# Seven first products by Strassen's scheme, and forward transforms of 512 columns, in an H3 and MLP kernel

## The chip, the cores and the metric

The kernel runs on one core of a Trainium2 chip. The metric is the device time of one execution in microseconds (us). Before the change it is 848.18 us, the median of three runs (847.58 to 848.95).

## The reference

A sequence of 2048 tokens with 640 features passes four layers: a gated long convolution (A), an MLP (B), then both again with the same weights.

```python
def _A_ref(q, k, v, shift_k, ssm_k, ssm_D):
    ...
    kv = k_shift * v                      # k_shift: short causal convolution of k, 4 taps
    ...
    y = (lambda x, s, axes=(-2,-1): jnp.fft.irfft2(x, s=s, axes=axes))(y_f, (1, L), axes=(1, 2))[:, 0, :S, :]
    y = y + kv * ssm_D[None, None, :]
    return q * y

def _B_ref(x, w1, w2):
    h = jnp.einsum("bsd,df->bsf", x, w1)
    zero = jnp.zeros_like(h)
    h = jnp.maximum(h, zero)
    return jnp.einsum("bsf,fd->bsd", h, w2)

x = A_q
x = x + _A_ref(_layernorm(x, axis=-1), A_k, A_v, A_shift_k, A_ssm_k, A_ssm_D)
x = x + _B_ref(_layernorm(x, axis=-1), B_w1, B_w2)
x = x + _A_ref(_layernorm(x, axis=-1), A_k, A_v, A_shift_k, A_ssm_k, A_ssm_D)
x = x + _B_ref(_layernorm(x, axis=-1), B_w1, B_w2)
```

w1 is 640 by 1728, w2 1728 by 640. The convolution of A has no state that depends on x, so its result y is the same in both A layers and is computed once.

## The kernel before

**MLP blocks.** Tokens go in eight chunks of 256 (NC = 8). A block (a, l) is the MLP of chunk a in layer l. `order` lists them: chunks 0 and 1 in halves of 128 tokens, then in pairs of chunks, so that the last four blocks are (6,0), (7,0), (6,1), (7,1). `prep` makes a block's input (two layernorms, gate with y, residual), splits it into a high and a low f16 part (tile `xh`) and transposes both by DMA on the SP queue into `xT` (L1149). `main` runs over seven pairs of 128 hidden features (NFP = 7, in the order JS = 0, 1, 2, 3, 6, 4, 5). For a pair j the first product (`mm1`, L1291 to L1294) takes three f16 matmuls for each of the five feature tiles and each half of the pair: w high on x high, w high on x low, w low on x high; 30 matmuls of 256 columns into one PSUM tile `h` (ring of two). ACT applies the relu and DVE makes the low part of the result. The second product of the pair before is issued behind the first product of this one (`second(*prev)`). In the last four blocks (WINO) the second product already follows Strassen's scheme in Winograd's form: `wprod` (L1214), seven products of 320 columns on sums of h (`ha`, `hs`, `gs`, `tp`) and on combined forms of w2 that `wcombine` makes from w2 once more loaded. `wplain` is the plain form, used for j = 6 and, at some places, for one more pair.

**Convolution.** 21 units of one or two feature tiles. `transform(u)` loads k, v and the filter, applies taps and gate (tile `acc`), makes sum and difference `sd`, transposes on PE (`pt`), and multiplies by cosine and sine matrices (`pr`, L700 or L464 to L466); the filter goes the same way (`pg`). Units of rank FA = 6 and above (15 of them) do `pr` in three passes on a high and a low part in a rounded f32 type (`mm3`); the filter does so from rank FG = 11 on, and `products` (`pq`) from FU = 7 on. `products(u)` multiplies and adds spectra of earlier chunks, read back from DRAM (`Ax`, `Gx`), on DVE (L790 to L794), transforms back and writes y. The last unit's DVE instruction at L884 also writes `gate`, a tile without data: instructions that read it wait until the convolution is over and its buffers are free.

**Order.** Nothing is issued as written. `Plan` collects every instruction with a cost and a class, schedules them on a model of the engines and queues, computes latest start times (`latest`) and repeats the scheduling with them; MOVES is a list of passes, each of which is either empty (compute latest times again) or a tuple that shifts the keys of some instructions by pseudo-random amounts. The order that comes out is fixed for every engine and for SP. Buffers are rings: a tile takes the next free buffer of its tag.

Of the kernel before, what the change touches and what calls it, by code (L numbers as in the profile page):

```python
# [21 lines left out]
P = 128  # L22
# [64 lines left out]
FG = 11  # L87
# [5 lines left out]
SIGNED = ()  # L93
# [8 lines left out]

PETAP = {}

ACTN = 3
SADD0 = 0
WINO = ((6, 0), (7, 0), (6, 1), (7, 1))
EARLY = 1
ONPOOL = ()


def fview(ap):
    return ap.bitcast(F32)

# [15 lines left out]
class Sub:  # L130
# [5 lines left out]
    @property  # L136
    def t(self):
        return self.view(self.parent.t)


class Ring:
    def __init__(self, pool, tag, bufs):
# [1471 lines left out]
```

## Time and profile before

| | |
|---|---|
| runs before, median (range) | 848.18 us (847.58 to 848.95) |
| span of the profiled execution | 849.9 us |
| mean granted TensorE clock | 0.997 |
| busy: PE, DVE, ACT | 838.4, 754.0, 494.9 us |
| PE instructions | 7761 matmuls, as many weight loads |
| HBM | 183 GB/s over the span |

The span is from the first to the last instruction of one execution. No time other than the span is shown of that execution; it is 1.7 us longer than the median of the runs. A line such as L1291 is a line of the kernel before. Sums of matmul durations are larger than the time that they take, since a matmul's duration reaches into the next one; the distance from start to start is what PE needs for it.

The page's slices of the span (each 21.2 us, digits are tenths):

```profile
PE   7999999999999999999999998999999999999998
DVE  6999999999999999999999998999889598755454
ACT  4898597447685756637467373564516386647331
```

### The profile page before, as it was taken

How to read it: one execution, taken by the hardware profiler on the slowest of the kernel's cores; microseconds unless marked ns; L12 is line 12 of the kernel's file. 1: busy time of each engine (PE TensorE's matmuls, PEld its weight loads, DVE VectorE, ACT ScalarE, POOL GpSimd, SP SyncE). 2: the span in 40 equal slices, each digit the busy share in tenths (PEclk: the TensorE clock that was granted, in tenths of full speed). 3: DMA queues.
4: the chain of work that ended last, by engine and by line, in shares of the span. 5: the costliest groups of instructions: out<-in, count | busy, mean ns of one | idle time of the engine just before them, and what ended most of it. 6: DMA issues, size and time to landing. Idle time of an engine off the chain costs nothing.

```text
span 849.9 us, 19692 instructions
## 1 busy us (share of the span) xinstructions
PE 838.4 (99%) x7761; PEld 667.5 (79%) x7761; DVE 754.0 (89%) x1423; ACT 494.9 (58%) x1152; POOL 43.8 (5%) x54
## 2 busy tenths in 40 slices
PE   7999999999999999999999998999999999999998
PEld 6987888888878777777777776777777788888886
DVE  6999999999999999999999998999889598755454
ACT  4898597447685756637467373564516386647331
POOL 0000000000001101001011001010100000000000
PEclk9999999999999999999999999999999999999999
DMA  9996867987999998986998969597886363110100
GB/s 304 391 329 205 259 200 229 282 306 217 328 286 268 293 271 233 267 245 190 260 261 196 255 199 178 154 210 253 251 257 228 107 200 79 32 32 1 33 32 32
DMA packets 134143, 177.47 MB, mean 209 GB/s; under 512 B 50593, under 2 KB 88097, under 8 KB 134050
## 3 DMA queue, kind: packets, MB, share of 16 engines
q1 hardware_dynamic: 125730, 165.72, 63.7%
q0 software_dynamic: 8320, 10.49, 8.2%
q8 instruction: 61, 1.00, 0.5%
q14 instruction: 32, 0.26, 0.1%
HBM read 121.44 MB, written 34.08 MB: 183 GB/s over the span
## 4 chain that ended last, share of the span: by engine, by line
PE 89%; DVE 5%; DMA 2%; ACT 1%; SPq 1%; issue 1%; DVEq 0%
PE h L1291 12%; PE h L1292 12%; PE h L1294 12%; PE o L1214 9%; PE o L1263 8%; PE o L1264 8%; PE o L1266 7%; PE oc L1263 2%; PE oc L1264 2%; PE oc L1266 2%; PE pg L659 1%; PE pq L845 1%; DMA hf<-in_hF 1%; DVE w L975 1%; PE hb L1291 1%; PE hb L1292 1%
## 5 line engine op out<-in xcount | busy, mean ns | idle before, releaser
L1292 PE MATMUL h<-xT,w 128*128 128x256 f16 (+1 forms) x1290 | 302.1, 252 | 2.4 <-DMA xT<-xh 2.4
L1291 PE MATMUL h<-xT,w 128*128 128x256 f16 (+1 forms) x1290 | 302.2, 252 | 0.0
L1294 PE MATMUL h<-xT,w 128*128 128x256 f16 (+1 forms) x1290 | 302.0, 252 | 0.0
L1292 PEld LDWEIGHTS <-w 128*128 128x128 f16 x1390 | 136.3, 98 | 22.9 <-DMA xT<-xh 2.7
L1291 PEld LDWEIGHTS <-w 128*128 128x128 f16 x1390 | 136.3, 98 | 21.7 <-issue 0.5
L1294 PEld LDWEIGHTS <-w 128*128 128x128 f16 x1290 | 126.5, 98 | 9.1
L794 DVE TENSOR_TENSOR pacc<-pacc,pd 128x768 f32<-128x768 f32 x140 | 132.6, 948 | 0.4
L1263 PE MATMUL o<-w,hh 128*128 128x512 f16 x336 | 127.3, 379 | 0.0
L1264 PE MATMUL o<-w,hh 128*128 128x512 f16 x336 | 127.3, 379 | 0.0
L1380 ACT ACTIVATE hh<-h 128x512 f16<-128x512 f32 (+1 forms) x98 | 47.2, 484 | 119.3 <-PE h L1294 112.3
L1264 PEld LDWEIGHTS <-hh 128*128 128x128 f16 x672 | 65.8, 98 | 26.8 <-issue 0.3
L1263 PEld LDWEIGHTS <-hh 128*128 128x128 f16 x672 | 65.7, 98 | 26.8 <-issue 0.2
L793 DVE TENSOR_TENSOR pd<-Ax,Gx 128x768 f32<-128x768 f32 x83 | 78.2, 948 | 1.6 <-DMA Gx<-G 1.5
L1266 PE MATMUL o<-w,hl 128*128 128x512 f16 x208 | 78.8, 379 | 0.0
L1263 PE MATMUL oc<-w,hh 128*128 128x128 f16 x336 | 73.9, 220 | 0.0
L1264 PE MATMUL oc<-w,hh 128*128 128x128 f16 x336 | 73.6, 219 | 0.1
L1266 PEld LDWEIGHTS <-hl 128*128 128x128 f16 x416 | 40.7, 98 | 24.5
L538 ACT ACTIVATE tp<-kt,shs 128x256 f32<-128x256 f32 (+1 forms) x78 | 42.9, 575 | 12.9 <-DVE acc L612 10.3
L1266 PE MATMUL oc<-w,hl 128*128 128x128 f16 x208 | 45.6, 219 | 0.0
L1381 DVE SCALAR_TENSOR_TENSOR hl<-h,hh 128x512 f16<-128x512 f32 x50 | 34.2, 683 | 11.5 <-ACT hh L1380 11.5
L793 DVE TENSOR_TENSOR pd<-at,Gx 128x768 f32<-128x768 f32 x46 | 43.2, 948 | 1.3 <-DMA Gx<-G 1.1
L1266 PE MATMUL o<-w,hh 128*128 128x512 f16 x104 | 39.4, 379 | 0.0
(247 smaller groups left out, 1748.4 us busy)
## 6 DMA issues: line engine op xcount, KB each, us to landing
Ax<-A SPq DMA_DIRECT2D x89, 384.0 KB, 4.5
Gx<-G SPq DMA_DIRECT2D x89, 384.0 KB, 4.5
A<-at SPq DMA_DIRECT2D x30, 384.0 KB, 5.4
G<-gt SPq DMA_DIRECT2D x30, 384.0 KB, 4.9
ws<-in_w SPq DMA_DIRECT2D x28, 320.0 KB, 6.5
y<-Y SPq DMA_DIRECT2D x22, 320.0 KB, 4.0
x<-in_q SPq DMA_DIRECT2D x16, 320.0 KB, 4.5
gs<-in_hF SPq DMA_DIRECT2D x20, 256.0 KB, 3.9
```

What stands on the lines that cost most here:

```text
L538: ACT.activation(o[:, i : i + m], kview(i, m, j), AF.Copy, scale=shs[:, t, j : j + 1])
L793: ew(f"mac{j % POOLMOD}", 768, lambda e, pd=pd, av=av, gv=gv: e.tensor_mul(pd.t, av(), gv()), [ax, gx], [pd], pr_)
L794: dve(768, lambda i=i, pd=pd: DVE.tensor_add(acc[:, i], acc[:, i], pd.t), [acc, pd], [acc], pr_)
L1214: PE.matmul(b[:, c : c + w], x, y[:, z : z + w], start=done[i] == 1, stop=end, skip_group_check=fin)
L1263: PE.matmul(z, hh[:, c], wh[:, d], start=(j == JS[0] and i == 0 and (h == 0 or s == S[0])), stop=False)
L1264: PE.matmul(z, hh[:, c], wl[:, d], start=False, stop=end and tail)
L1266: PE.matmul(z, hl[:, c], wh[:, d], start=False, stop=end)
L1291: PE.matmul(p[:, z], wh, xv(t, 0), start=b, stop=False)
L1292: PE.matmul(p[:, z], wh, xv(t, 1), start=False, stop=tail and e)
L1294: PE.matmul(p[:, z], wl, xv(t, 0), start=False, stop=e)
L1380: act(2 * R, lambda p=p, hh=hh: ACT.activation(hh.t, p.t, AF.Relu), [p], [hh], URGENT)
L1381: dve(2 * R, lambda p=p, hh=hh, hl=hl: DVE.scalar_tensor_tensor(hl.t, p.t, 0.0, hh.t, op0=ALU.max, op1=ALU.subtract), [p, hh], [hl], URGENT)
```

## The change

1. **First product.** For blocks (6,1) and (7,1) (`WINO1`) and the pairs of `J1` (4, 5, 3, 1, 2; in (6,1) only 4 and 5), `wfirst` takes the place of the two `mm1` calls. Tokens (two halves of 128), hidden features (two of 128) and input features (two of 256) form a 2 x 2 x 2 product done in seven products of 128 columns; the fifth feature tile is added in plain form. 54 matmuls of 128 columns go into two `h` tiles, and one ACT copy and five DVE additions recombine them into an SBUF tile `both`, from which the relu then reads.
2. **Forms of w1.** `w1combine`, called behind `wcombine`, loads the five pairs of w1 again (ten DMAs of 320 KB that wait for `gate`), combines them on DVE, scales and splits them on ACT and DVE into tiles that take over buffers of the finished convolution (`SLOTS`).
3. **Forms of x.** `prep` of these two blocks makes four combined token tiles on DVE, splits them and transposes them by four more DMAs into `tT` (in `kt`, `vt`, `hf`, `hr`). The partial sums of the second product move from these to `pacc`; `hs` and `ls` become halves of one tile in `gs`.
4. **Forward transforms.** In the three-pass form the matrices are reordered so that the two that differ by alternating signs share one weight: the signs are put on the moving columns (ACT copies scaled by `alt`), and 6 matmuls of 512 columns take the place of 12 of 256. On ACT one copy of 512 becomes six of 256, on the way out two copies of 512 become two of 256 and one of 512 (a third copy of 512, of some units, becomes two of 256); on DVE one subtraction of 512 becomes two of 256.
5. **FG from 11 to 9**: two more units' filter transforms take the three-pass form.
6. **Waits and buffers.** In block (6,0) the plain second products and the relu also wait for `gate`. `cM` is split for four matrices, not six, and sits, like `cG`, in a ring. The unused code for signed units goes, with its load `cN`.
7. **MOVES** is another list, longer (311 shifts for 86), so the whole order is planned anew.

```diff
-FG = 11
+FG = 9
+WINO1 = ((6, 1), (7, 1))
+J1 = (4, 5, 3, 1, 2)
+J1_AT = {(6, 1): (4, 5)}
+SLOTS = (("cs", 2), ("cs", 2), ("cg", 1), ("dl", 1), ("acc", 1), ("tp", 2), ("tp", 2), ("u", 2), ("u", 2), ("ag", NAG))
...
+            xh, xl = (T(cv, "rt", 2, [P, 2, h], f"s{x}" + nm, F32R) for x in "hl")
+            yh, yl = (T(cv, *r_, [P, 2, h], f"d{x}" + nm, F32R) for r_, x in ((("tp", 2), "h"), (("dl", 1), "l")))
+            for hi, lo, k in ((xh, xl, 0), (yh, yl, 1)):
+                act(h, lambda hi=hi, k=k: ACT.activation(hi[:, k], pv()[:, k], AF.Copy), [pt], [hi], pr_)
+                dve(h, lambda hi=hi, lo=lo, k=k: DVE.tensor_sub(lo[:, k], pv()[:, k], fview(hi[:, k])), [pt, hi], [lo], pr_)
+            for hi, k in ((xh, 1), (yh, 0)):
+                act(h, lambda hi=hi, k=k: ACT.activation(hi[:, k], pv()[:, k], AF.Copy, scale=alt.t), [pt, alt], [hi], pr_, 0.09)
+            for lo, src, k in ((xl, yl, 1), (yl, xl, 0)):
+                act(h, lambda lo=lo, src=src, k=k: ACT.activation(lo[:, k], fview(src[:, k]), AF.Copy, scale=alt.t), [src, alt], [lo], pr_, 0.09)
+
+            def f():
+                for i, (hi, lo) in enumerate(((xh, xl), (yh, yl))):
+                    mm3(pr[i][:, 0:w], cMs, i, hi.r("p a b -> p (a b)"), lo.r("p a b -> p (a b)"), True, True)
...
+    def w1combine():
...
+            dve(256, lambda b=b: DVE.tensor_add(b(1, 1), b(1, 1), b(1, 0)), [r1], [r1], CONV)
+            dve(256, lambda b=b: DVE.tensor_sub(b(1, 0), b(0, 0), b(1, 0)), [r0, r1], [r1], CONV)
+            dve(256, lambda b=b: DVE.tensor_sub(b(0, 0), b(1, 1), b(0, 0)), [r0, r1], [r0], CONV)
+            dve(256, lambda b=b: DVE.tensor_sub(b(0, 1), b(0, 1), b(0, 0)), [r0], [r0], CONV)
+            dve(P, lambda b=b: DVE.tensor_sub(b(0, 2), b(0, 2), b(1, 2)), [r0, r1], [r0], CONV)
...
+                act(512, lambda r=r, w=w: ACT.activation(w[:, 0], r[:, 0:512], AF.Copy, scale=s()), [r, sc[0]], [w], CONV, 0.09)
+                dve(512, lambda r=r, w=w: DVE.scalar_tensor_tensor(w[:, 1], r[:, 0:512], s(), w[:, 0], op0=ALU.mult, op1=ALU.subtract), [r, sc[0], w], [w], CONV, 0.13)
...
-                pe(0.136 * (6 if j < NFP - 1 else 5), f, [hh, hl, WT[j, 1, 0], WT[j, 1, 1]], [b for b, *_ in place(m)], FILL + 0.2 * ending)
+                pe(0.136 * (6 if j < NFP - 1 else 5), f, [hh, hl, WT[j, 1, 0], WT[j, 1, 1]] + [gate] * ((a, layer) == WINO[0]), [b for b, *_ in place(m)], FILL + 0.2 * ending)
...
+        def wfirst(j, pa, pb, c):
...
+            groups = (
+                (A, 0, ((plain_w(0, 0), tok(0, 0), 2),)),
+                (A, 1, ((form(f0, 0), comb(1), 2),)),
+                (A, 2, ((form(f1, 1), comb(0), 2), (a_(1), tail_x(1), 1))),
+                (A, 3, ((form(f1, 0), comb(2), 2),)),
+                (B, 0, ((form(f0, 1), tok(1, 1), 2), (ad, tail_x(1), 1))),
+                (B, 1, ((plain_w(1, 1), comb(3), 2), (a_(1), tail_x(0), 1))),
+                (B, 2, ((plain_w(0, 1), tok(0, 1), 2), (a_(0), tail_x(0), 1))),
+            )
...
+                    mms = [(w(kk, h), x(kk, l)) for w, x, n_ in parts for kk in range(n_) for h, l in ((0, 0), (0, 1), (1, 0))]
+                    for z, (y, x) in enumerate(mms):
+                        PE.matmul(p[:, k * P : k * P + P], y, x, start=z == 0, stop=z == len(mms) - 1)
...
+            act(P, lambda: ACT.activation(c[:, 3], at_(A, 0), AF.Copy), [A], [c], URGENT)
+            dve(P, lambda: DVE.tensor_add(c[:, 0], at_(A, 1), c[:, 3]), [A, c], [c], URGENT)
...
+            dve(256, lambda: DVE.tensor_add(c[:, 1:3], at_(A, 2, 2).rearrange("p (k e) -> p k e", k=2), once()), [A, c], [c], URGENT)
+            dve(P, lambda: DVE.tensor_add(c[:, 0], at_(B, 2), c[:, 3]), [B, c], [c], URGENT)
+            dve(P, lambda: DVE.tensor_add(c[:, 3], at_(A, 2), c[:, 2]), [A, c], [c], URGENT)
+            dve(256, lambda: DVE.tensor_add(c[:, 1:3], at_(B, 0, 2).rearrange("p (k e) -> p k e", k=2), c[:, 1:3]), [B, c], [c], URGENT)
...
-            mm1(j, 0, p)
-            p1 = T(ps, "h", 2, [P, 2 * R], f"hb{n}", stream=sm) if j == NFP - 1 else p
-            mm1(j, 1, p1)
+            seven = tT is not None and j in J1_AT.get((a, layer), J1)
+            if seven:
+                p1 = T(ps, "h", 2, [P, 2 * R], f"hs{n}_{j}", stream=sm)
+                both = T(cv, "rt", 2, [P, 4, P], f"ha{n}_{j}", stream=7)
+                wfirst(j, p, p1, both)
```

More of the change, by code (lines that the diff above doesn't have):

```diff
@@ L456, in csplit @@
     def csplit(t, k, ring=None, after=()):
-        hi, lo = (T(wp, "w", NW, [P, k, P], t.name + x, F32R, stream=2) if ring else keep(const, [P, k, P], t.name + x, F32R) for x in "hl")
-        act(k * P, lambda: ACT.activation(hi.t, t.t, AF.Copy), [t, *after], [hi], LATER)
-        dve(k * P, lambda: DVE.tensor_sub(lo.t, t.t, fview(hi.t)), [t, hi], [lo], LATER)
+        hi, lo = (T(*ring, [P, k, P], t.name + x, F32R, stream=2) for x in "hl")
+        act(k * P, lambda: ACT.activation(hi.t, t[:, 0:k], AF.Copy), [t, *after], [hi], LATER)
+        dve(k * P, lambda: DVE.tensor_sub(lo.t, t[:, 0:k], fview(hi.t)), [t, hi], [lo], LATER)
         return hi, lo
@@ L686, in transform @@
         pv = lambda: pt[:, 0:w].rearrange("p (a b) -> p a b", a=2)
-        sh = T(cv, "rt", 2, [P, 2, h], "sh" + nm, F32 if full else F32R)
-        act(w, lambda: ACT.activation(sh.t, pv(), AF.Copy), [pt], [sh], pr_)
-        if not full:
-            sl = T(cv, "rt", 2, [P, 2, h], "sl" + nm, F32R)
-            dve(w, lambda: DVE.tensor_sub(sl.t, pv(), fview(sh.t)), [pt, sh], [sl], pr_)
         at = T(*park, [P, n, 3, 256], "at" + nm, stream=1)
         pr = [R(f"p{ri}", [P, 512], f"pr{ri}" + nm) for ri in range(2)]
-        def f(ris):
-            for ri in ris:
+        third = by_dma and not c0
@@ L697, in f @@
+        if full:
+            sh = T(cv, "rt", 2, [P, 2, h], "sh" + nm)
+            act(w, lambda: ACT.activation(sh.t, pv(), AF.Copy), [pt], [sh], pr_)
+            def f(ri):
                 for kk in range(2):
                     o = pr[ri][:, 0:w].rearrange("p (c k e) -> p c k e", c=n, k=2)[:, :, kk, :]
-                    if full:
-                        PE.matmul(o, cMt[:, 2 * kk + ri, :], sh[:, ri, :], start=kk == 0, stop=kk == 1)
-                    else:
-                        mm3(o, cMs, 2 * kk + ri, sh[:, ri, :], sl[:, ri, :], kk == 0, kk == 1)
@@ L704, in transform @@
-        if full:
-            for ri in range(2):
-                pe(8 * mm4, lambda ri=ri: f([ri]), [sh, cMt], [pr[ri]], pr_)
-        else:
-            pe(12 * mm, lambda: f([0, 1]), [sh, sl, *cMs], pr, pr_)
-        for ri in range(2):
-            act(w, lambda ri=ri: ACT.activation(at[:, :, ri, :], pr[ri][:, 0:w].rearrange("p (c b) -> p c b", c=n), AF.Copy), [pr[ri]], [at], pr_)
-        if by_dma and not c0:
-            act(w, lambda: ACT.activation(at[:, :, 2, :], pr[0][:, 0:w].rearrange("p (c b) -> p c b", c=n), AF.Copy), [pr[0]], [at], pr_)
+                    PE.matmul(o, cMt[:, 4 * kk + ri, :], sh[:, ri, :], start=kk == 0, stop=kk == 1)
@@ L1322, in main @@
         if wino:
-            e1, u2, u3, v = (T(cv, x, 1, [P, H], f"e{x}{n}", stream=7) for x in ("kt", "vt", "hf", "hr"))
+            kept = T(cv, "pacc", 1, [P, 4, H], f"ek{n}", stream=7)
+            e1, u2, u3, v = (Sub(kept, lambda t, k=k: t[:, k]) for k in range(4))
             def res(s, h, src, t, z=0, w=H, last=False):
@@ L1547, in _consts @@
     cg = np.concatenate([cg, -cg[:, 2:4], -cg[:, 1:2]], 1)
-    cg = np.concatenate([cg, -cm[:, 1:2], -cm[:, 5:6]], 1)
-    return [x.astype(np.float32) for x in (cm, cg)]
+    return [x.astype(np.float32) for x in (cm, cg, row)]
 def _rows(x):
```

151 lines of the change are left out of this document (109 added, 42 removed), and 70 rows, old and new, of the table MOVES.

## The prediction

> **What bounds the kernel now.** I read the page's totals first, then a table of busy time by stretch, then the order of the matmuls one by one in the few places where the change puts its hand.
>
> ```profile
> span 849.9 us, 19692 instructions
> PE 838.4 (99%) x7761; PEld 667.5 (79%) x7761; DVE 754.0 (89%) x1423; ACT 494.9 (58%) x1152; POOL 43.8 (5%) x54
> ```
>
> A busy PE need not be a full PE, since its instructions overlap, so I counted steps from start to start. In the plain first product of the last blocks 60 matmuls of 256 columns lie between these two starts (the row behind them ends a full second product):
>
> ```profile
> 804.44 0.27 PE L1291 MATMUL h<-xT,w 128*128 128x256 f16 x1
> ...
> 810.99 0.43 PE L1214 MATMUL o<-w,hh 128*128 128x320 f16 x2
> ...
> 813.85 0.27 PE L1291 MATMUL h<-xT,w 128*128 128x256 f16 x1
> ```
>
> 6.55 us / 60 = 0.1092 us each, and the seven 320-column products that follow take 2.86 us. PE issues without a hole. The stretches say the same (from:to, length, then PE, PEld, DVE, ACT, POOL busy):
>
> ```profile
> 100.00:650.00 550.00, 547.23 (x5063) 426.56 (x5061) 534.49 (x905) 321.28 (x763) 41.96 (x40) 1.00 0.88 246
> 676.00:720.00 44.00, 44.00 (x407) 37.43 (x405) 37.23 (x84) 32.23 (x70) 0.00 (x0) 1.00 0.54 162
> 720.00:803.00 83.00, 83.00 (x745) 69.46 (x744) 49.24 (x140) 46.33 (x111) 0.00 (x0) 1.00 0.11 25
> 803.00:846.00 43.00, 42.75 (x379) 35.38 (x377) 22.62 (x57) 11.14 (x21) 0.00 (x0) 1.00 0.06 20
> ```
>
> From 100 us on PE sets the end. DVE is nearly full too up to 650 us (534.5 of 550) and has room only in the last four blocks. PE's one large hole behind the start is here:
>
> ```profile
> 517.80 0.81 DVE L1137 TENSOR_TENSOR xh<-xnB,xh 128x640 f16<-128x640 f32 x1
> 519.61 7.28 DMA xT<-xh
> 526.94 0.28 PE L1292 MATMUL h<-xT,w 128*128 128x256 f16 x1 [2.35 <-DMA xT<-xh]
> 527.00:529.00 2.00, 2.00 (x14) 1.59 (x15) 1.45 (x5) 0.00 (x0) 0.00 (x0) 0.72 0.62 208
> 529.00:531.00 2.00, 2.00 (x12) 1.41 (x10) 0.00 (x0) 0.00 (x0) 0.00 (x0) 0.50 0.00 0
> ```
>
> The block at 524 us has its input split late on the full DVE (517.80), the transposing DMA lands 7.28 us later, PE idles 2.35 us, and then the granted clock (the seventh figure behind the length) is 0.72 and 0.50. A mean of 0.72 is 1.12 of 2 us at half rate; with the 2 us behind it that is 3.1 us at half rate, 1.6 us lost. The hole costs 2.35 + 1.6 = 3.9 us. The Trainium skill ("TensorE: Matmul & The Clock Gate", part 1 on the HAM clock gate) has the clock halved only after an idle window of about 3.4 us; this trace differs, 2.35 us of idleness was enough here. By the page the hole would be worth 2.35 us alone.
>
> **The change, part by part.** PE first.
>
> First product of seven feature pairs (two in block (6,1), five in (7,1)). Removed: 30 matmuls of 256 columns, 30 x 0.1092 = 3.28 us. Added: 54 of 128 columns (27 into each of two PSUM tiles). Their step stands in the half blocks, where the same pattern (two streams on one weight, then the low weight) runs 30 at a time:
>
> ```profile
> 163.68 0.38 PE L1264 MATMUL o<-w,hh 128*128 128x512 f16 x1
> 163.90 0.38 PE L1266 MATMUL o<-w,hh 128*128 128x512 f16 x1
> 164.11 0.22 PE L1291 MATMUL h<-xT,w 128*128 128x128 f16 x1
> ...
> 165.73 0.22 PE L1294 MATMUL h<-xT,w 128*128 128x128 f16 x1
> 165.76 0.36 PE L464 MATMUL pr<-sh,cMh 128*128 128x256 f32 x1
> 165.96 0.29 PE L465 MATMUL pr<-sl,cMh 128*128 128x256 f32 x1
> ...
> 167.16 0.28 PE L466 MATMUL pr<-sh,cMl 128*128 128x256 f32 x1
> 167.28 0.23 PE L1263 MATMUL oc<-w,hh 128*128 128x128 f16 x1
> ```
>
> 29 steps in 1.62 us: 0.0559 each, 54 make 3.02 us. 7 x 0.26 = **1.8 us less**. It is near one tenth of the multiplications, since the fifth tile of features keeps its plain form, and twice as many instructions each carry about 3 ns.
>
> The Trainium skill speaks against this part: the same page, section "Back-to-back issue gap", gives 81 ns for a sustained stream of weight load and matmul at 128 columns, far over the 56 of one matmul alone. The row above disagrees: it is such a stream, each matmul with its own load, at 56. By the page 54 would be 4.4 us, an estimate, and each pair a loss of 1.1.
>
> Forward transforms. The group from 165.76 to 167.28 is the old form: 12 matmuls of 256 columns, 1.52 us, 0.120 a step from 165.96 on, and 0.08 more on the first. The new form is 6 of 512 over the same columns. No such row with this type exists. From below it is the f16 step at 512 columns (163.68 to 163.90: 0.215), from above twice the old step (0.240). I take 0.22, nearer the lower, because in f16 doubling the columns halves the fixed part. That is 0.08 + 6 x 0.22 = 1.40, 0.12 less (0 to 0.15). It runs in 15 units:
>
> ```profile
> L464 PE MATMUL pr<-sh,cMh 128*128 128x256 f32 x60 | 18.8, 313 | 0.0
> 78.07 1.95 PE L659 MATMUL pg<-gs,cG 128*128 128x256 f32 x8
> 79.85 0.22 PE L1263 MATMUL oc<-w,hh 128*128 128x128 f16 x1
> ```
>
> (60 of this kind, four a unit.) 15 x 0.12 = **1.8 us less** (0 to 2.2). FG from 11 to 9 moves two units' filter transform from 8 full-precision matmuls (78.07 to 79.85: 1.78 us) to the 12-matmul form (1.52): **0.5 us less**.
>
> Now what the other engines get. DVE and ACT, by start-to-start steps and means:
>
> ```profile
> 513.13 0.68 DVE L691 TENSOR_TENSOR sl<-pt,sh 128x512 fp32r<-128x512 f32 x1
> 513.73 0.94 DVE L794 TENSOR_TENSOR pacc<-pacc,pd 128x768 f32<-128x768 f32 x1
> ...
> 641.07 0.41 DVE L883 TENSOR_TENSOR ys<-pq,qs 128x256 f32<-128x256 f32 x1
> 641.40 0.95 DVE L794 TENSOR_TENSOR pacc<-pacc,pd 128x768 f32<-128x768 f32 x1
> ...
> 665.88 0.68 DVE L852 TENSOR_TENSOR ul<-u,uh 128x512 fp32r<-128x512 f32 x1
> 673.56 0.47 PE L464 MATMUL pq<-uh,cMh 128*128 128x256 f32 x1
> 676.14 0.41 DVE L884 TENSOR_TENSOR ys<-pq,qs 128x256 f32<-128x256 f32 x1
> ```
>
> On DVE each of the 15 units trades a 512 subtraction (0.60) for two of 256 (0.33 each): +0.06 x 15 = 0.9. FG adds 2 x 2 x 0.60 = 2.4. So 3.3 us more before the convolution ends. The cover: the last unit's operands are ready at 665.88 + 0.60 = 666.5 and PE takes them at 673.56, 7.1 us later, because it still has block (5,1) to do. PE will be there 2.3 us sooner and DVE 3.3 later; 1.5 us are left, so I cost it at nothing. Were the cover gone, the gate (written at 676.14) would be late, and with it three engines' queues: on SP the w2 and w1 loads and behind them the inputs of (7,0); on ACT the relu of (6,0)'s second pair and behind it the copies that its split needs; on PE the second product of its first pair and behind it the next first product. PE would idle by as much as the gate is late, each microsecond one for one, and by 1.6 more once it has idled 2.35.
>
> ```profile
> L880 ACT ACTIVATE qs<-pq 128x256 f32<-128x256 f32 x19 | 7.2, 376 | 17.8 <-PE pq L466 17.2 <-PE pq L845 0.5
> L710 ACT ACTIVATE at<-pr 128x512 f32<-128x512 f32 x38 | 22.1, 587 | 10.5 <-PE pr L466 5.9 <-PE pr L700 4.1
> ```
>
> On ACT a unit had one copy in and two out (3 x 0.59 = 1.8 us). It gets six of 256 in, two of 256 and one of 512 out (8 x 0.376 + 0.59 = 3.6): +27 us over 15 units, +2 for the third part of ten of them, +2.5 for FG. ACT goes from 321 to about 352 of 550 us, and these copies are behind no matmul that is due at once; nothing, as long as the order keeps the relus of the MLP first.
>
> The last four blocks. The forms of w1 cost DVE, per pair, four passes of 256, one of 128, two scalings of 512, one of 128; a prep with tT four of 256 and two of 512; the recombination three of 128 and two of 256:
>
> ```profile
> 815.68 0.60 ACT L1367 ACTIVATE ha<-h 128x512 f32<-128x512 f32 x1 [1.87 <-PE h L1294]
> 816.31 0.29 DVE L1371 TENSOR_TENSOR hs<-ha 128x128 f32<-128x128 f32 x1 [1.78 <-ACT ha L1367]
> ...
> 818.65 0.69 DVE L1378 TENSOR_TENSOR tp<-hs,gs 128x512 f16<-128x512 f32 x1 [0.69 <-ACT gs L1376]
> ...
> 840.30 0.69 DVE L1381 SCALAR_TENSOR_TENSOR hl<-h,hh 128x512 f16<-128x512 f32 x1 [2.52 <-ACT hh L1380]
> 840.91 0.48 DVE L1340 TENSOR_TENSOR evt<-o,ekt 128x320 f32<-128x320 f32 x1
> ```
>
> With 0.41, 0.29 and 0.69: 4 x 0.41 + 0.29 + 2 x 0.69 + 0.29 = 3.6, times five 18.0; preps 2 x 3.0 = 6.0; recombination 1.7 a pair, 3.4 in (6,1) and 8.5 in (7,1). From 720 to 803 us that is 27.4 us into 83 - 49.2 = 33.8 us of room; in the last block 8.5 into 20.4. The ten loads and eight transposes meet an almost idle DMA (share 0.11), and on SP they stand ahead only of the other transposes of a block that starts some 40 us later. The chain behind a first product, relu to last low part, is now 815.68 to 819.34, 3.7 us; three DVE passes more behind the second PSUM tile make it 4.7. It is needed after the second product before it (2.86) and the next first product (3.02), 5.9 us later: covered, with 1.2 us over. Its two PSUM tiles come free about 1 us behind their last matmul, inside those 2.86.
>
> The end: there DVE runs one pass after another from 840.30. Three passes more (1.0 us) fall just before, where it has 2.5 us idle, but the low part of the last pair comes 1 us later and pushes what follows. I take **+0.2 us** (0 to +0.8).
>
> The sum is -1.8 - 1.8 - 0.5 + 0.2 = -3.9 us on a span of 849.9: 846.0. The median of the runs lies 1.7 us under that span, what lies around the span included; carried over, 848.18 - 3.9 = **844.3 us**.
>
> **The rivals.** The whole order is planned anew, so the hole at 524 us is not bound to return, and another can open.
>
> *No hole.* The new order brings that block's split before 515 us, or the landing is short. Then another 3.9 us go: 840.4. For it: one late DVE pass and one slow landing made it. Against: DVE gets fuller in that stretch, and the runs' median, 1.7 us under the profile, may lack part of it already. Chance 0.21.
>
> *One hole more.* Where DVE is full, another block's input or the gate comes 2.4 us late: +3.9, 848.2, no change. For it: 1.5 us of cover left before the gate. Chance 0.17.
>
> *DVE takes over in the last blocks* (the other side). It decides from the point where forms, splits and recombinations together outrun the 33.8 us of room between 720 and 803: at 27.4 added DVE would be 92% full there, and a recombination queued behind a 0.69 scaling or two is late by more than the 1.2 us that its chain has over. If each of the seven pairs makes PE wait by one form pass and its hop, about 0.8, plus one half-clock spell of 1.6, the cost is 7.2: 848.18 - 3.9 + 7.2 = 851.5. Against: before 650 us the kernel runs at 97% DVE with one hole. Chance 0.13.
>
> *Weight loads bind the 128-column stream.* A load takes 98 ns:
>
> ```profile
> L1292 PEld LDWEIGHTS <-w 128*128 128x128 f16 x1390 | 136.3, 98 | 22.9 <-DMA xT<-xh 2.7
> ```
>
> At one per load 54 make 5.3 us, +2.0 a pair, 14 in all: 848.18 + 14 - 2.1 = 860. That is how the skill's 81 ns would act; the rows at 164 us speak plainly against it. Chance 0.02.
>
> **How the numbers follow.** My forecast, the arithmetic with the waits as they are, has 0.47; its own range is 842.5 (transforms at their best, half a hole less) to 846.4 (transforms gain nothing). The range 839.9 to 849.2 takes in the case without a hole and that with one more, and leaves the two slow cases out. 0.2% is 1.7 us, about what a measurement of this kernel tells from no change, so faster is under 846.5: 0.47 + 0.21 = 0.68. Within: 0.17. Slower: 0.15.
>
> **What would show it.** Steps right: 54-matmul groups at 0.056 a step; pr groups of six at 0.21 to 0.24; pg groups of eight in two units fewer; PE without idle rows between 676 us and the end, DVE there above 85%. Wrong: PE idle rows in front of o or h matmuls released by DVE in the last two blocks, or by xT or tT landings; a half clock behind them; a pq group of the last unit that follows its ul pass at once, which says that the cover at the gate is gone.

## The result, and the profile after

| | before | after |
|---|---|---|
| runs, median (range), 22 each | 848.42 us (846.89 to 851.91) | 849.44 us (848.04 to 852.50) |
| ratio to before, 95% interval | | 1.0016 (1.0009 to 1.0024) |
| span of the profiled execution | 849.9 us | 847.2 us |
| that execution's own time | not known | 849.02 us |

The change costs 1.0 us; 844.3 was forecast. The two profiled spans say the opposite of the runs, and the reason comes first. Every listed execution of these two kernels that has both figures has its time 1.7 to 1.9 us over its span (849.02 over 847.2 here). The median of the runs before, 848.42, belongs to a span near 846.6. The profiled execution of before, at 849.9, was some 3 us longer than the usual one, so its hole at 524 us can hardly be in most runs (an inference: only profiled executions show their waits).

The lines of the page after, and the stretches of the trace (from:to, length, then PE, PEld, DVE, ACT, POOL busy, granted clock, DMA share, GB/s):

```profile
span 847.2 us, 20204 instructions
PE 835.9 (99%) x7847; PEld 661.0 (78%) x7847; DVE 788.2 (93%) x1529; ACT 534.3 (63%) x1282; POOL 43.8 (5%) x54
DVE  7999999999999999999999999999998789989775
ACT  4898687557785666667466466564725377678531
100.00:650.00 550.00, 545.94 (x4978) 418.31 (x4976) 535.71 (x919) 347.98 (x865) 42.02 (x40) 1.00 0.87 243
720.00:803.00 83.00, 83.00 (x808) 70.54 (x807) 71.22 (x202) 57.43 (x134) 0.00 (x0) 1.00 0.29 66
803.00:843.00 40.00, 40.00 (x480) 34.29 (x477) 28.91 (x79) 10.91 (x23) 0.00 (x0) 1.00 0.06 22
```

The last blocks look much as forecast: PE never idles, and DVE is 86% full from 720 to 803 us (71.22 of 83), where 92% was forecast. In the middle, from 100 to 650 us, ACT has risen from 321 to 348 us, DVE is as full as before, and PE idles 4.1 us instead of 2.8. The waits of PE (engine, line, what it waited for; us in total, times, longest), without those of the start:

```profile
PE h L1378 <- DMA xT<-xh: 2.4, 3, 1.1
...
PE pt L726 <- ACT ob L706: 0.7, 1, 0.7
PE h L1377 <- DVE hh L1535: 0.5, 1, 0.5
...
```

The first row is three inputs of blocks, at 320, 476 and 527 us. The chain that leads to the one at 476 us (start, us, what), and the matmul that waited:

```profile
464.89 0.75 DVE xh L1206
465.64 0.60 DVE gt L707
466.24 0.87 DVE pacc L853
467.11 0.60 DVE gt L708
467.71 0.73 DVE xh L1206
...
470.92 6.52 DMA xT<-xh
477.48 0.27 PE h L1378
```

```profile
476.09 0.28 PE L1377 MATMUL h<-xT,w 128*128 128x256 f16 x1
477.48 0.27 PE L1378 MATMUL h<-xT,w 128*128 128x256 f16 x1 [1.11 <-DMA xT<-xh]
```

DVE runs one pass after another and has split the block's second token half only at 468.4 us, the last transpose of it lands 9.0 us later, and the second matmul of the block has to wait. Its start is 1.39 us behind the first instead of 0.11: the wait costs 1.28 us. The same reading gives 0.9 at the transposes at 319 us (late on ACT), 0.7 at 321, 0.9 at 527 and 0.6 at 232 us. None of these holes in the middle was followed by a half clock.

The two products that were to become cheaper, in the order of the matmuls (a row with x12 stands for twelve in succession). First one half of a Strassen product and the row behind it; then one group of the forward transforms and the row behind it:

```profile
826.97 0.50 PE L1410 MATMUL h<-xT,w 128*128 128x128 f16 x6
827.31 0.83 PE L1410 MATMUL h<-tT,wf 128*128 128x128 f16 x12
827.98 0.33 PE L1410 MATMUL h<-xT,w 128*128 128x128 f16 x3
828.14 0.50 PE L1410 MATMUL h<-tT,wf 128*128 128x128 f16 x6
828.48 0.57 PE L1300 MATMUL o<-w,gs 128*128 128x320 f16 x3
```

```profile
201.46 0.48 PE L507 MATMUL pr<-sh,cMh 128*128 128x512 f32 x1
201.77 0.39 PE L508 MATMUL pr<-sl,cMh 128*128 128x512 f32 x1
...
202.94 0.23 PE L1533 MATMUL hb<-tb,down 128*128 128x128 f16 x1
```

27 steps take 1.51 us, 0.056 each, as predicted. The transform group takes 202.94 - 201.46 = 1.48 us, where 1.40 was forecast and the old form took 1.52 in the quoted group. The step is 0.234 in the mean (0.22 to 0.24), near the upper bound, and the first one 0.31.

### The profile page after: what moved, and what is told of

Read it like the earlier page. It is cut to its first block, busy times and chain, and to the rows that moved or that the text cites. A ratio compares the mean times of both kernels' runs of the same rounds, so it can differ in the third digit from the quotient of the medians.

```text
span 847.2 us, 20204 instructions
## 1 busy us (share of the span) xinstructions
PE 835.9 (99%) x7847; PEld 661.0 (78%) x7847; DVE 788.2 (93%) x1529; ACT 534.3 (63%) x1282; POOL 43.8 (5%) x54
## 4 chain that ended last, share of the span: by engine, by line
PE 75%; DVE 10%; DMA 7%; ACT 4%; issue 2%; SPq 1%; POOL 0%; DVEq 0%; ACTq 0%; POOLq 0%
PE h L1378 10%; PE h L1377 10%; PE h L1380 10%; PE o L1300 9%; PE o L1350 6%; PE o L1349 6%; PE o L1352 5%; DMA xT<-xh 3%; PE pg L679 2%; PE oc L1349 2%; PE oc L1350 2%; PE oc L1352 1%; PE hs L1410 1%; PE h L1410 1%; DMA Y<-ys 1%
## 5 line engine op out<-in xcount | busy, mean ns | idle before, releaser
L1378 PE MATMUL h<-xT,w 128*128 128x256 f16 (+1 forms) x1220 | 282.0, 250 | 2.5 <-DMA xT<-xh 2.4
L1377 PE MATMUL h<-xT,w 128*128 128x256 f16 (+1 forms) x1220 | 282.2, 250 | 0.6 <-DVE hh L1535 0.5
L1380 PE MATMUL h<-xT,w 128*128 128x256 f16 (+1 forms) x1220 | 282.0, 250 | 0.0
L1377 PEld LDWEIGHTS <-w 128*128 128x128 f16 x1320 | 129.1, 98 | 21.0 <-issue 2.0
L1378 PEld LDWEIGHTS <-w 128*128 128x128 f16 x1320 | 129.2, 98 | 19.6 <-issue 0.8
L1380 PEld LDWEIGHTS <-w 128*128 128x128 f16 x1220 | 119.4, 98 | 10.5 <-issue 2.5
L1349 PE MATMUL o<-w,hh 128*128 128x512 f16 x336 | 127.3, 379 | 0.0
L1350 PE MATMUL o<-w,hh 128*128 128x512 f16 x336 | 127.3, 379 | 0.0
L603 POOL DMA_DIRECT2D gs<-hr x20 | 18.4, 918 | 412.3 <-DVE dl L753 219.1
```

The costliest lines, as they stand in the source:

```text
L1349: PE.matmul(z, hh[:, c], wh[:, d], start=(j == JS[0] and i == 0 and (h == 0 or s == S[0])), stop=False)
L1350: PE.matmul(z, hh[:, c], wl[:, d], start=False, stop=end and tail)
L1377: PE.matmul(p[:, z], wh, xv(t, 0), start=b, stop=False)
L1378: PE.matmul(p[:, z], wh, xv(t, 1), start=False, stop=tail and e)
L1380: PE.matmul(p[:, z], wl, xv(t, 0), start=False, stop=e)
```

## Experiments in new orders: too coarse

Two theories. *A*: the matmul saving is real, and the order that comes with the change gives it back by chance. *B*: the added work on ACT and DVE makes inputs late in any order. Each variant was therefore given an order of its own, planned anew by the same search of the same length for each, so that no kernel got more of the search than another.

First the kernel before again, and both kernels without any shifts, one execution each:

```diff
-MOVES = ((),) * 4 + ((...), ...)
+MOVES = ((),) * 4 + ()
```

> The kernel before, unchanged, profiled a second time. Its first profile had a span of 849.9 us, but the runs' median less about 1.8 us (the distance of time and span in the listed runs of the kernel after) says that a usual execution has 846.6. If the hole at 524 us was a chance of that execution, the span is 845.5 to 847.5 and PE's waits behind 60 us sum to 1 us or so; if the order itself holds the hole, it is there again and the span is 849 to 850. The theories on the change (A: it saves some 2 us of PE work and the new order gives them back in waits at block starts between 230 and 530 us, for reasons of the order; B: the added work of VectorE and ScalarE in the stretch where VectorE is full makes such waits in any order) both expect the first.

> The kernel before with the list of shifts of the planner emptied, the four passes on latest times left. It tells what the list is worth. Both theories expect it slower than 848.4 us; A, that the order is what decides, expects 5 us or more, by waits of PE on xT and on VectorE's parts.

> The kernel after with the list of shifts emptied in the same way. If the change is worth about 2 us of PE work whatever the order (A), this is 1 to 4 us faster than the kernel before with the list emptied, give or take the chance that each order brings; if the added VectorE and ScalarE work binds in any order (B), it is not faster.

Measured: 850.4 (beside another execution of the same kernel at 848.05), 858.26 and 857.13. The shifts are worth some 10 us to the kernel before and 8 to the changed one. Without them the change is 1.1 us faster, but these are single executions. Neither branch of the first expectation came in whole: the span, 848.6, lies between the two, and the hole of before was there again, smaller:

```profile
525.55 0.27 PE L1291 MATMUL h<-xT,w 128*128 128x256 f16 x1
527.30 0.28 PE L1292 MATMUL h<-xT,w 128*128 128x256 f16 x1 [1.48 <-DMA xT<-xh]
```

Then orders of equal effort, for both kernels and for each half of the change:

```diff
-MOVES = ((),) * 4 + (...)
+MOVES = ((),) * 4 + (another list, found by the same search)
```

```diff
 # first_only_eq: old transforms, old FG, one slot in another ring
-FG = 9
+FG = 11
...
-SLOTS = (..., ("cg", 1), ("dl", 1), ...)
+SLOTS = (..., ("cg", 1), ("ag", NAG), ...)
...
-                    mm3(pr[i][:, 0:w], cMs, i, hi.r("p a b -> p (a b)"), lo.r("p a b -> p (a b)"), True, True)
+                        mm3(o, cMs, 4 * kk + ri, sh[:, ri, :], sl[:, ri, :], kk == 0, kk == 1)
...
```

```diff
 # trans_only_eq: no Strassen in the first product
-WINO1 = ((6, 1), (7, 1))
+WINO1 = ()
...
-                    w1combine()
```

> The kernel before with another list of shifts, found by one search of 25 minutes that is run in the same way for this and the three programs that follow, so that all four are planned with the same effort. It is the yardstick for the other three. Both theories expect 848 to 850 us and PE waits behind 60 us of 1 to 4 us.

> The kernel after, planned with the same effort. A (the loss is one of the order it was given, the change itself saves 2 us of PE work): about 2 us faster than the kernel before planned in the same way. B (the added work of VectorE and ScalarE makes waits of PE at block starts in any order): no faster than that one, with 3 us or more of PE waits between 230 and 530 us.

> The seven first products by Strassen's scheme alone: forward transforms in their old form of 12 matmuls of 256 columns, and the filter form from rank 11 on as before; one of the buffers of the forms of w1 is another, since one ring is gone. Planned with the same effort. Both: PE work 1.8 us under the kernel before. B: no added load in the middle, so waits there as in the kernel before planned in the same way, and 1.5 to 2 us faster than it. A: the same 2 us, no better than the whole change planned in this way.

> The forward transforms of 512 columns and the filter form from rank 9 on alone, plain first products everywhere. Planned with the same effort. In the trace of the kernel after a group of six 512-column matmuls takes 1.56 us where the old 12 took 1.52, so PE work falls by 0.5 (filters) and rises by 0.6 at most. A: as the kernel before planned in this way, within 1 us. B: 1.5 us or more slower than it, with PE waits between 230 and 530 us of 3 us or more.

And, later, four more: Strassen with only one of the two other edits, and a second, independent search for the kernel before and for Strassen alone.

```diff
 # fg11_eq: the whole change without its FG
-FG = 9
+FG = 11
```

> Strassen's products and the new forward transforms, FG back at 11, in an order of its own found with the same search time as the others. B-T (the ACT copies of the transforms cost the waits): as slow as the whole change, 849.5 to 851, PE waits behind 60 us together 4 to 6 us between 100 and 530 us. B-F (the DVE work of FG costs them): near Strassen alone, 846 to 848, waits together under 3 us. A (chance of the order): neither binds, 846 to 851.

> Strassen's products and FG at 9, with the old forward transforms, in an order of its own of the same search time. B-T: near Strassen alone, 846 to 847.5 (FG saves 0.5 us of PE), waits together under 3 us. B-F: 848.5 to 850.5; the 2.4 us of DVE work come back as waits of 2 us or more. A: neither binds, 846 to 851.

> Strassen's products alone, in a second order from another start of the search. Where the gain is its own: 845.5 to 848, below the kernel before by 1 to 3 us, as in its first order (846.85). A, that the first order was a lucky one: 848 to 851.

> The kernel before in a second order from another start of the search. Where an order of this search time on the kernel before is worth what its own order is: 847.5 to 850, and the first one (851.83) was an unlucky one. Where the kernel's own order is better than this search finds: 850 to 853. The difference between this and 851.83 is the spread by the order alone; if it is over 2 us, A can't be excluded for any single pair.

Measured (4 to 10 executions each: median, range, ratio to the kernel before on the same chip with its interval):

| kernel | order | us | ratio |
|---|---|---|---|
| before | search 1 | 851.83 (849.72 to 858.25) | 1.0047 (1.0026 to 1.0069) |
| before | search 2 | 858.38 (856.87 to 859.60) | 1.0121 (1.0104 to 1.0138) |
| whole change | search 1 | 850.27 (849.12 to 853.11) | 1.0027 (1.0013 to 1.0041) |
| Strassen alone | search 1 | 846.85 (845.61 to 847.42) | 0.9976 (0.9965 to 0.9986) |
| Strassen alone | search 2 | 852.03 (851.73 to 853.46) | 1.0050 (1.0035 to 1.0065) |
| transforms and FG alone | search 1 | 850.14 (848.61 to 852.71) | 1.0023 (1.0009 to 1.0038) |
| Strassen and transforms | search 1 | 848.73 (847.68 to 850.83) | 1.0005 (0.9994 to 1.0016) |
| Strassen and FG | search 1 | 850.31 (848.69 to 853.04) | 1.0030 (1.0015 to 1.0044) |

One kernel, before, takes 848.4, 851.8 or 858.4 us by its order alone; Strassen alone takes 846.9 or 852.0. The spread by the order is several times what is looked for. Within one search every changed kernel came out faster than before, and Strassen alone gained 5.0 and 6.4 us, more than its matmuls save, so most of that is order too. No pair of this table can be read as the price of an edit. It does not decide between *A* and *B*, nor between the transforms and FG. It gives one kernel that beats both, Strassen alone in its first order. The middle of its profiled execution, the fastest of its ten:

```profile
100.00:650.00 550.00, 549.54 (x5098) 428.34 (x5096) 537.88 (x909) 320.69 (x762) 42.16 (x40) 1.00 0.87 248
```

0.5 us of idle PE in the middle, with DVE at 98%: a full DVE does not by itself make holes. What a bad order does is seen in the second one of before, one block input 4 us late and a half clock behind it (stretches below):

```profile
270.93 0.38 PE L1879 MATMUL o<-w,hh 128*128 128x512 f16 x1
275.04 0.37 PE L1904 MATMUL h<-xT,w 128*128 128x256 f16 x1 [3.73 <-DMA xT<-xh]
```

```profile
274.00:276.00 2.00, 0.96 (x5) 0.74 (x6) 1.65 (x3) 0.00 (x0) 0.00 (x0) 0.74 1.06 328
276.00:278.00 2.00, 2.00 (x12) 1.39 (x11) 0.00 (x0) 0.00 (x0) 0.91 (x1) 0.50 1.04 383
```

## Experiments in one fixed order

What tells parts apart is one order kept instruction for instruction, with only the contents of single instructions altered. First, work added to Strassen alone (846.85), as much as the transforms and FG add. The repeated instructions write the same values again.

```diff
 # load_act: three more copies of 512 columns in each of the 15 units
-            act(w, lambda: ACT.activation(sh.t, pv(), AF.Copy), [pt], [sh], pr_)
+            act(w, lambda: [ACT.activation(sh.t, pv(), AF.Copy) for _ in range(4)], [pt], [sh], pr_)
 # load_dve: the DVE work of the change
-            dve(w, lambda: DVE.tensor_sub(sl.t, pv(), fview(sh.t)), [pt, sh], [sl], pr_)
+            dve(w, lambda: [DVE.tensor_sub(sl[:, k], pv()[:, k], fview(sh[:, k])) for k in range(2)], [pt, sh], [sl], pr_)
...
-            dve(w, lambda: DVE.tensor_add(gt[:, :, 0:2, 0, :], e4(pg[0]), ob.t), [pg[0], ob], [gt], pr_)
+            dve(w, lambda: [DVE.tensor_add(gt[:, :, 0:2, 0, :], e4(pg[0]), ob.t) for _ in range(again)], [pg[0], ob], [gt], pr_)
...
```

> The kernel with the Strassen first products alone, in exactly its own order (846.85 us), with ScalarE's part of the new transforms' load added and nothing else: in each of the 15 units the copy of 512 columns into the high part is made four times, three of 0.59 us more, 27 us in all; the result is the same. B (the added work makes the waits): slower by 1 us or more, with PE waits behind 60 us above the 1.5 us that its own profile has, if ScalarE's share of the load matters. A (only the order matters): 846.8, within 0.7 us.

> The same kernel and order with VectorE's part of the added load alone: the two passes of the filter result of units 9 and 10 made twice (2 x 2 x 0.6 = 2.4 us) and the low part of the 15 units made in two passes of 256 in place of one of 512 (0.9 us). B: slower by 1 to 3 us, with the waits of PE at block starts between 230 and 530 us, as VectorE is full there. A: 846.8, within 0.7 us.

> The same kernel and order with both loads. B: slower by the sum of the two, 2 to 4 us, about where the whole change planned with the same effort stands (850.3). A: 846.8, within 0.7 us.

Measured: 860.14 (1.0125, 1.0097 to 1.0154), 848.53 (0.9999, 0.9985 to 1.0012) and 862.51 (1.0154, 1.0129 to 1.0179). 3.3 us on DVE cost 1.7 us (846.85 to 848.53; the executions range from 845.61 to 847.42 and from 847.84 to 849.58). 27 us on ACT, of which the pages show 25 (507.4 to 532.5), cost 13 us. "Off the critical path" does not mean free here: ACT is 60% busy in Strassen alone and still has no slack where the work was put.

The DVE part came back at another place than its expectation said. Lined up matmul by matmul with the profile of Strassen alone, PE falls 3.0 us behind between 180 and 217 us and loses nothing more from there to the end (that profile was the fastest of its ten). 2.3 us of it are waits for `hh`, which here holds the low part of a relu and stands on DVE behind the doubled passes:

```profile
178.67 1.41 DVE L1265 TENSOR_TENSOR gt<-pg,ob 128x512 f32<-128x512 f32 x2
...
180.71 0.28 DVE L2084 SCALAR_TENSOR_TENSOR hh<-hb,hh 64x128 f16<-64x128 f32 x1
```

```profile
181.06 0.23 PE L1898 MATMUL oc<-w,hh 128*128 128x128 f16 x1 [0.73 <-DVE hh L2084]
```

PE's largest waits under the ACT load, and then one of DVE's, which Strassen alone does not have:

```profile
PE oc L1900 <- DVE hl L2069: 2.2, 2, 1.4
PE h L1926 <- DMA xT<-xh: 2.2, 2, 1.1
```

```profile
DVE sl L1307 <- ACT sh L1306: 14.3, 12, 1.9
```

PE waits behind DVE and its transposes more than behind ACT: the low part of a unit has to wait for the last of four copies, and so DVE is late. The size does not carry over to the change, though, because its planner knew of the copies and laid them around the relus, and this order did not.

The last four go at the changed kernel in its own order (849.44) and, for contrast, at the kernel before in its own.

```diff
 # after_plain: the seven Strassen products plain again, in the same places
...
-                        PE.matmul(p[:, k * P : k * P + P], y, x, start=z == 0, stop=z == len(mms) - 1)
+                        PE.matmul(p[:, 0 : 2 * P], y, xT[0, x][:, t, :], start=t == 0 and z == 0, stop=t == NDT - 1 and z == 2)
...
-            dve(P, lambda: DVE.tensor_add(c[:, 0], at_(A, 1), c[:, 3]), [A, c], [c], URGENT)
+            dve(P, lambda: DVE.tensor_copy(c[:, 1], at_(A, 1)), [A, c], [c], URGENT)
...
 # after_split: 12 matmuls of 256 columns for 6 of 512
-                    mm3(pr[i][:, 0:w], cMs, i, hi.r("p a b -> p (a b)"), lo.r("p a b -> p (a b)"), True, True)
+                    for k in range(2):
+                        z = slice(k * h, k * h + h)
+                        mm3(pr[i][:, z], cMs, i, hi[:, k], lo[:, k], True, True)
 # after_less, before_less: six accumulations cut to one column
-            dve(768, lambda i=i, pd=pd: DVE.tensor_add(acc[:, i], acc[:, i], pd.t), [acc, pd], [acc], pr_)
+            def add(i=i, pd=pd):
+                n = 1 if len(count) in LESS else 768
+                count.append(0)
+                DVE.tensor_add(acc[:, i, 0:n], acc[:, i, 0:n], pd[:, 0:n])
+
+            dve(768, add, [acc, pd], [acc], pr_)
```

> The changed kernel in its own order, with the seven Strassen products replaced by plain ones (30 matmuls of 256 columns each) in the same places, and the recombination by copies of the same sizes. If the saving counts in full in this order: 7 x 0.26 = 1.8 us slower than the changed kernel, 851.2 (850.8 to 851.8), and no new waits in the last two blocks. If the last blocks are set by DVE or by the end of the last block instead: no difference, 849.4.

> The changed kernel in its own order, with each 512-column matmul of the forward transforms as two of 256 (12 a group, as before; same result). By the prediction's term of 0.12 us a group: 15 x 0.12 = 1.8 slower, 851.2. By the groups as they stand in the profile (1.56 against 1.52): 0.04 x 15 = 0.6 faster, and less where the next wait swallows it, 848.8 to 849.5.

> The changed kernel in its own order, six DVE accumulations of 768 columns cut to one column, two ahead of each of the block inputs at 320, 476 and 527 us (5.4 us of DVE work left out, and with it six terms of the convolution's sums). If these inputs are late on DVE: the three waits of 0.7, 1.3 and 0.9 us go, and the time falls by 2 to 3.5 us, to 846 to 847.5. If the landing of their transposes or the chance of the order sets them: the waits stay, 849 to 849.6.

> The kernel before in its own order, with the same cut at the same block inputs. If late inputs on DVE are in the kernel before too (its hole at 524 us): 1.5 to 3 us less than 848.4, 845.5 to 847. If the change made them: under 1 us, 847.4 to 848.4, and clearly less than in the changed kernel's order.

Measured:

| kernel | us | ratio to before |
|---|---|---|
| changed kernel | 849.44 | 1.0016 (1.0009 to 1.0024) |
| after_plain | 850.46 (848.85 to 853.30) | 1.0022 (1.0007 to 1.0037) |
| after_split | 848.39 (846.40 to 849.56) | 0.9996 (0.9982 to 1.0010) |
| after_less | 847.30 (846.34 to 849.46) | 0.9985 (0.9972 to 0.9998) |
| before_less | 847.90 (847.08 to 850.49) | 0.9997 (0.9984 to 1.0011) |

**after_plain.** The medians differ by 1.0 and the ratios by 0.0006, which is 0.5 us (the changed kernel's runs stand beside runs of before at 848.42, these beside 848.06). The intervals overlap, and the middle differs from execution to execution by as much. The trace is sharper. The last unit's `pq` marks the end of the middle, and behind it PE runs nearly without a hole to the end. The same matmul in the changed kernel, and then in after_plain with its span:

```profile
676.26 0.36 PE L507 MATMUL pq<-uh,cMh 128*128 128x256 f32 x1
```

```profile
674.74 0.36 PE L507 MATMUL pq<-uh,cMh 128*128 128x256 f32 x1
```

```profile
core 0: 847.6 us, clock 0.999
```

From there to the end: 847.2 - 676.26 = 170.94 us with Strassen and 847.6 - 674.74 = 172.86 without, a difference of 1.9 us for seven pairs, in one execution of each. The saving is real and arrives at the end in full. What is lost is lost before 676 us.

**after_split.** The group of the quoted place, now in twelve:

```profile
201.40 0.36 PE L507 MATMUL pr<-sh,cMh 128*128 128x256 f32 x1
...
202.92 0.23 PE L1535 MATMUL hb<-tb,down 128*128 128x128 f16 x1
```

1.52 us against 1.48. Over all 15 groups, each from its first matmul to the next matmul behind it, twelve take 23.55 us and six 22.95: merging saves 0.6 us of PE time, a third of the 1.8 forecast. The expectation had the groups the wrong way round, 1.56 for the merged form; group for group in one order it is 1.53 against 1.57 in the mean. And the kernel with the slower groups was not slower but 1.0 us faster in its median, with intervals that just touch. That this time comes from shorter waits fits its trace, which has only 0.2 us of `xT` waits left:

```profile
PE h L1380 <- DMA xT<-xh: 0.2, 1, 0.2
```

**after_less and before_less.** The waits of the changed kernel with 5.4 us less DVE work ahead of three block inputs, and the stretch from 100 to 650 us; then that stretch of the kernel before with the same cut:

```profile
PE pt L727 <- ACT ob L707: 0.7, 1, 0.7
...
PE h L1383 <- DVE hh L1541: 0.5, 1, 0.5
PE h L1384 <- DMA xT<-xh: 0.4, 2, 0.2
```

```profile
100.00:650.00 550.00, 548.32 (x4996) 420.05 (x4993) 533.77 (x923) 347.88 (x865) 42.09 (x40) 1.00 0.86 243
```

```profile
100.00:650.00 550.00, 547.96 (x5085) 426.82 (x5083) 532.27 (x909) 321.37 (x763) 41.98 (x40) 1.00 0.89 247
```

With the cut, the changed kernel's three waits on `xT` are gone, down from 2.4 to 0.4 us (what is left lies behind 700 us), PE idles 1.7 us in that stretch instead of 4.1, and the time falls by 2.1 us to 847.30, with the intervals apart. The waits that are not behind DVE's splits, on `ob` and `hh`, stay. In the kernel before the same cut brings 848.06 (its runs beside it) to 847.90, nothing that can be told.

That these inputs are late because of DVE does not follow, though. The trace of after_split, where DVE does all its work, lacks the same three waits, and its time, 848.39, has an interval that overlaps that of after_less, whose profiled execution, 846.34, is also the fastest of its ten. And ahead of the input at 476 us the cut freed 1.6 us on DVE, but DVE spent most of it waiting, at last for ACT, right before the first split of that input:

```profile
463.57 0.82 DVE L1212 TENSOR_TENSOR xh<-xnB,xh 128x640 f16<-128x640 f32 x1 [0.51 <-ACT xh L1211]
```

The wait at an input can be taken apart. Call *cover* the time from the end of DVE's last split of the input to the point where PE asks for it, and *landing* the time from the same end until the last transpose has landed. PE waits by what the landing has over the cover. From the traces, in us:

| input at | execution | cover | landing | PE waits, start to start |
|---|---|---|---|---|
| 476 us | changed kernel | 7.75 | 8.99 | 1.28 |
| | after_plain | 7.76 | 6.80 | 0 |
| | after_split | 7.78 | 7.88 | 0.15 |
| | after_less | 7.75 | 5.22 | 0 |
| 524 us | before | 5.81 | 8.28 | 2.51 |
| | before again | 5.81 | 7.41 | 1.64 |
| | before_less | 5.82 | 3.33 | 0 |

At these two inputs the cover is the same in every execution of an order, with the DVE work cut or not; the landing differs by 4 to 5 us, and by 2 us between the changed kernel and after_plain, whose instructions are the same up to there. So it is the landing that made and unmade these two waits. At the inputs at 321 and 528 us the cut did widen the cover, by 0.6 and 0.7 us, but the landings were 1.8 and 3.4 us shorter than in the changed kernel's profile as well. What makes a landing long, and whether less DVE work shortens it, was not found out. What the cut shows is that 2.1 us of the changed kernel's time can be had in the middle, not that DVE's lateness is what takes them.

## Why the prediction was wrong, point by point

**First product: right.** 1.8 us forecast, 1.9 measured in one fixed order; 0.056 a step. Nothing is left of the rival in which weight loads bind the 128-column stream. The 81 ns of the Trainium skill ("TensorE: Matmul & The Clock Gate", section "Back-to-back issue gap") did not appear either.

**Last four blocks: right.** 22 us more DVE work lie between 720 and 803 us (71.22 for 49.24), less than the 27.4 forecast; PE has no idle there, and DVE did not take over. The end brought no visible loss: it is contained in the 1.9.

**The gate: right, but not by its sum.** It had 7.1 us of cover, and 1.5 were to be left, with PE there 2.3 us sooner. After, the last two `ul` passes are done at about 672.4 us and PE takes them at 676.46: 4 us are left, since PE came there 2.7 us later than in the profile before (676.26 for 673.56).

**Forward transforms: mis-sized.** This term was put at 1.8 us, with a step of 0.22, because in f16 doubling the columns halves a fixed part. By the prediction's own rows that part is small: two steps of 0.1092 less one of 0.215 are 3 ns, and 3 ns off the upper bound of 0.240 are 0.237, not 0.22. The step measured 0.234, and merging saves 0.6 us. Splitting them again did not slow the kernel, so even the 0.6 were not seen in the time.

**The step that failed: the added DVE work (3.3 us) and ACT work (31 us) in the middle, costed at nothing.** The cover was examined at one place, the gate, because that is where the convolution ends, and for ACT it was argued. But DVE and ACT also make the input of every block and both parts of every relu, and there PE takes them with little cover or none. In place of nothing the runs show a price: the DVE part alone, put into one fixed order, cost 1.7 us, and the ACT part 13. The changed kernel's loss is in the middle too: PE idles 4.1 us there, 1.3 more than in the profiled execution before, though that one was a long one, and cutting DVE work ahead of three block inputs gives 2.1 us back, in the changed kernel only. In sums: 848.4 - 1.9 for the first products - 0.6 at most for the transforms - 0.5 for FG (forecast, not measured by itself) is 845.4; the runs say 849.4. Of the 4.0 between them, after_less gets 2.1 back, but after_split, without any cut, gets 1.0, and the traces put both down to landings for the larger part; the waits on `ob` and `hh` (0.9 and 0.6 by start-to-start distance) stand in all four traces of this order. That is where the loss lies. Why this order has it is not shown.

**The rivals.** *One hole more* named the place, another block's input, and nearly the right size of loss, 3.9 us; but the loss came as half a dozen waits of 0.3 to 1.3 us, without a half clock. *No hole* named the short landing, which before_less then had (3.33 us, no hole at 524), but counted on a gain that the median, as far as the runs tell, already had. The 1.7 us between span and median were carried over as a constant, when they were the sign that the profiled execution had the hole and most runs, by their times, had not: time lies 1.8 us over the span, not under it.

**Open.** Whether the waits in the middle come from the added work or from an order that happened to lay it badly: the load runs show that such work costs in an order that was not planned for it (0.5 us a us on DVE), the searches show that an order can move the time by 5 us and more, and no run separates the two for this change. What makes a transpose land 5 or 9 us after its split is open too. Lightening ACT in the changed kernel's order was not tried.

## What to carry to other kernels

When an engine is nearly full, look for the cover of added work at every place where it hands something to the bounding engine, not only at the last; room on average and cover at one place say nothing of the others. A part's worth is measured in a fixed order, by altering what instructions do and not where they stand; an order planned anew moved this kernel by more than the whole change. Before putting a wait for a transpose down to the engine that made its input late, split it into cover and landing and compare executions of the same order: the cover belongs to the order, the landing here did not. And compare the profiled span with the runs before pricing a hole in it: the hole may be that execution's own.

## What the hardware showed unexpectedly

How long PE may idle before its clock halves lies between 1.6 and 2.1 us in these traces, behind their first 20 us. Holes of 1.34 (Strassen and transforms, 527 us), 1.48 (before again, 527 us), 1.56 (second order of before, 220 us) and 1.61 us (transforms and FG alone, 112 us) were followed by full clock, holes of 2.09 us (whole change, search 1, 322 us) and more by half clock. Two holes with little between them seem to count together: 0.75 and 1.53 us with four matmuls between (changed kernel without shifts, 323 us), and in the second order of Strassen alone 1.65 and 0.28 us with one matmul between:

```profile
478.75 0.28 PE L1889 MATMUL h<-xT,w 128*128 128x256 f16 x1 [1.65 <-DMA xT<-xh]
479.31 0.28 PE L1890 MATMUL h<-xT,w 128*128 128x256 f16 x1 [0.28 <-DMA xT<-xh]
```

```profile
479.00:481.00 2.00, 1.72 (x12) 1.33 (x12) 2.00 (x4) 0.47 (x1) 0.72 (x1) 0.72 1.01 404
481.00:483.00 2.00, 2.00 (x11) 1.42 (x10) 0.96 (x2) 0.15 (x1) 0.00 (x0) 0.50 1.19 273
```

Clocks of 0.72 and 0.50 (the seventh figure behind the length), with 0.93 in the slice behind, make 3.4 us at half rate. The hole of 2.35 us before comes to the same with its third slice (0.93 from 531 to 533 us), where the prediction counted two slices and 3.1 us. The Trainium skill ("TensorE: Matmul & The Clock Gate", part 1 on the HAM clock gate) has about 3.4 us of idleness ahead of a half clock; of the holes followed by one here, only those of 3.73 and 3.85 us (before without shifts, 481 us) are as long. And the same order does not wait alike each time: the hole of before at 524 us was 2.35 and 1.48 us, and the wait of the changed kernel at 476 us, 1.28 us there, is not in after_plain, whose instructions are the same up to that point.
